# One 32-row product turned round: weights stationary in 128-column pieces instead of a product, a copy and four transposes

## The chip, the cores and the metric

One core of one Trainium2 chip runs the whole program. The metric is device time in microseconds of one execution; the kernel before took 707.13 us (median of three timed runs, 706.22 to 708.27). TensorE is written PE, its weight loads PEld, VectorE DVE, ScalarE ACT, GpSimd POOL and SyncE SP. SP issues all the transfers of this kernel.

## The reference

```python
def _attn_ref(x, state):                      # x (4, 8, 512, 64), state (4, 8, 32, 64)
    a = softmax(x @ state.T / 8);    xread = a @ state
    a2 = softmax(state @ x.T / 8);   sread = a2 @ x
    return concatenate([xread, sread], axis=2)          # 544 tokens for each of 4 batches
def _moe_ref(x, w_in, w_out, alpha):          # x (2176, 512), w_in (512, 2048), w_out (2048, 512)
    h = x @ w_in
    g = maximum(h, 0) + alpha * minimum(h, 0)
    return g @ w_out
def _moe2_ref(x, w_in, w_out):
    h = x @ w_in
    g = maximum(h, 0) + log1p(exp(-abs(h)))
    return g @ w_out
```

(The softmax lines are shortened.) The two stages are fed one from the other: attention, then stage 0 (with alpha), then stage 1. Each batch gives 512 token rows and 32 state rows; the state rows of the four batches together make one more block of 128 rows.

## The kernel before, in words

The work is cut by stage `m` (0 and 1), by quarter `q` of the 2048 hidden columns (512 each), by batch block `b` (0 to 3, 512 token rows each, and `b == B`, the 128 state rows), and by piece `fc` of 128 hidden columns. Most products are done three times on halves (`mm3`: high by high, high by low, low by high); some, the state rows' first product of stage 0 among them, are done once in full f32, which the trace shows as two passes for each matmul.

Stage 0 of the token blocks never multiplies `w_in` with the attention output. The product of state and `w_in` (`sw_products`, steps `w`) is made first and multiplied with the attention weights (`hidden` for `b < B`). For the state rows, `sr[0]` holds the 128 rows transposed, and their first product is with `w_in` itself (`whole(q, k)`, four row pieces `k`). The kernel before holds 128 columns of `sr` stationary and streams 512 columns of `w_in` (`hidden_rows`, L369). The result has tokens on its partitions, and the next product needs hidden columns there, so ACT copies it out (`rows_copy` L389, in quarter 0 step `J` L893), and PE transposes it in four pieces of 128 by 128 (`turned_rows` L397, in quarter 0 step `H` 16, by the helper at L633). Then `act` follows: a Relu on ACT (L413), `prelu` on DVE (L405), the split into halves (L184, L185). The second product of a block (`out_part`) runs three blocks later (`LAG = 3`).

Quarter 0 and the attention are written out by hand as the list `ORDER`: a letter is a step, a number its index, and every engine takes its own steps in the order of the list. The names that matter here: `N` filler transposes of the identity (L641), `L` loads of weights, `P` the load of alpha, `x` and `y` loads of the inputs `xt` and `xs`, `s` and `S` scores (L700), `b` 0 the transposition of group 0's weights (L633), `T`, `K`, `R`, `F`, `X` the state rows' own attention, `w` the products of state and `w_in` (L333), `H` first products, `A C G D` their activation. From quarter 1 on, Python loops write the order, and tables say beside which block further work is put: `TICKS` and `GROUP_TICKS` (conversion of one 128 by 512 weight tile: ACT L262 and L263, DVE L267 to L277, POOL L283, store and next load on SP), `W_AHEAD` and `Y_AHEAD` (preparation of stage 1). The second stage runs groups of seven products (`product`, L586).

The lines of quarters 1 to 3 around the state rows:

```python
for fc in range(4 if b < B else 1):
    hs = rows_copy(0, q) if b == B else None
    if n in TICKS[q]:
        conv_head()
    ps = hidden(0, q, b, fc) if b < B else turned_rows(hs, lambda: out_part(*todo.pop(0)))
    g = act(0, q, b, fc, ps)
    if len(todo) >= LAG:
        out_part(*todo.pop(0))
```

Of the kernel before, what the change touches and what calls it, by code (L numbers as in the profile page):

```python
# [49 lines left out]
b0 f1 x2 L4 Z0 N12 t1 v1 a2 j2 m1 f2 g1 x3 a3 K0 u1 N12 e1 v2 S2 j3 R0 z1 f3 r1 n1 L5 g2 k3 v3 k2 g3 N7 t2 B0 F0 w00  # L50
w01 t3 m3 b1 m2 a4 j4 e2 z2 u3 f4 p00 c0 e3 V0 X0 H0 r2 v4 p01 L6 a5 q01 n2 z3 g4 A0 W0 b2 j5 H1 c2 C0 d2 a6 A1 r3 h4
H3 d0 f5 H2 n3 G0 L7 N3 w03 C1 j6 G1 l4 L8 A2 c1 D0 D1 p03 x5 f6 C2 v6 v5 q03 b3 G2 A3 C3 c3 D2 g6 G3 g5 O0 D3 d3 w02
h5 p02 q02 d1 M2 x4 h6 a8 a7 j7 f7 M1 H5 l5 v7 S4 H4 E2 A4 j8 L9 A5 C5 C4 f8 y1 v8 O1 k4 M4 t4 E1 l6 g7 G4 k5 h7 l7 H6
D4 O2 G5 g8 y2 H7 L10 A6 a9 T2 T1 O3 D5 C6 j9 E4 m4 t5 m5 u5 f9 M5 v9 u4 a10 A7 Q3 e4 O4 z4 e5 r4 C7 z5 E5 K1 K2 O5 G6
Z2 r5 n4 R2 n5 Z4 D6 b4 M3 R1 T4 F2 Z1 F1 X2 b5 c5 c4 O6 W2 X1 y3 d4 G7 d5 Z5 E3 H8 x6 x7 W1 D7 j10 A8 f10 H9 K4 A9
L11 C8 T3 C9 G8 G9 K3 O7 Q7 S6 R3 Z3 H10 k7 D9 v10 T5 D8 t7 F3 m7 u7 k6 e7 X3 A10 t6 m6 O8 M6 K5 y4 L12 H11 y5 z7 C10
M7 u6 e6 W3 r7 E6 A11 G10 g10 g9 D10 R4 z6 r6 R5 F5 L13 n7 b7 O9 a11 C11 n6 c7 G11 b6 O10 F4 c6 a12 D11 y6 y7 L14 d6
T6 X5 W5 E7 j11 X4 f11 v11 d7 H12 g11 K6 H13 W4 A12 R6 a13 T7 A13 C12 Z7 j12 G12 Z6 C13 f12 O11 D12 H14 v12 G13 Q11
D13 g12 A14 F6 O12 H15 C14 j13 L15 G14 a14 K7 f13 X6 R7 W6 D14 h12 w11 F7 v13 j14 l12 g13 A15 a15 f14 C15 v14 j15 X7
L16 f15 W7 h13 O13 G15 g14 l13 O14 v15 D15 I0 w10 p11 J0 H16 A16 h14 g15 l14 q11 O15 C16 p10 q10 G16 D16 H17 L17 Q15  # L60
H18 A17 A18 O16 H19 w13 C17 h15 G17 C18 D17 G18 Q16 A19 H20 D18 O17 C19 G19 p13 A20 q13 w12 C20 D19 G20 p12 l15 D20
L18 q12
# [1033 lines left out]
```

## Time and profile before

| what | value |
|---|---|
| timed runs, median (lowest to highest) | 707.13 us (706.22 to 708.27) |
| the profiled execution, its own time | 705.88 us |
| span, first to last instruction of that execution | 704.1 us |
| busy: PE / PEld / DVE / ACT / POOL | 694.9 / 545.6 / 506.3 / 468.7 / 355.0 us |
| mean granted clock of TensorE | 1.000 of full speed |

The span is what the views of the trace divide up; 1.8 us lie around it. Busy time of PE counts pipelined matmuls with overlaps, so it says that PE has no long gaps and not that it is at its peak. The profiled execution is 1.25 us below the median.

### The profile page before, as it was taken

What the parts mean: (1) busy time and instruction counts of PE and PEld (TensorE: products, weight loads), DVE (VectorE), ACT (ScalarE), POOL (GpSimd) and SP (SyncE); (2) the same over time, 40 slices, a digit from 0 to 9 for tenths busy, and PEclk for the clock granted to TensorE, in tenths of its full rate; (3) what the DMA queues carried; (4) which work ended last, traced back from release to release, by engine and by line L of the source; (5) the groups of instructions that cost most, each with busy time, mean ns of one, the idle gap of its engine ahead of it and who ended that gap; (6) DMA issues with size and microseconds to landing.
All of it is one profiled execution on the core that took longest, in us unless ns stands there. A gap on an engine that the chain in (4) does not pass through costs nothing.

```text
span 704.1 us, 10175 instructions
## 1 busy us (share of the span) xinstructions
PE 694.9 (99%) x3512; PEld 545.6 (77%) x3512; DVE 506.3 (72%) x832; ACT 468.7 (67%) x921; POOL 355.0 (50%) x401
## 2 busy tenths in 40 slices
PE   8999999999999999999999999999999999999997
PEld 6468776777777777768888888888888888888886
DVE  5988876678999988887355666757676456677665
ACT  4878786646656566555589866757885776766551
POOL 2562323015234324548997684287997666554110
PEclk9999999999999999999999999999999999999999
DMA  8262712122543464664110423103105121200003
GB/s 301 104 208 86 237 45 85 60 89 89 184 133 119 137 220 145 202 198 147 30 61 13 167 75 106 45 1 103 47 31 168 58 89 31 91 30 31 0 31 119
DMA packets 30483, 72.47 MB, mean 103 GB/s; under 512 B 3552, under 2 KB 3552, under 8 KB 30432
## 3 DMA queue, kind: packets, MB, share of 16 engines
q1 hardware_dynamic: 30432, 71.83, 30.9%
q8 instruction: 27, 0.44, 0.3%
q14 instruction: 24, 0.20, 0.1%
HBM read 58.97 MB, written 12.85 MB: 102 GB/s over the span
## 4 chain that ended last, share of the span: by engine, by line
PE 92%; DMA 3%; DVE 1%; POOL 1%; ACT 1%; issue 1%; SPq 0%; POOLq 0%; ACTq 0%
PE pa L586 22%; PE pb L179 17%; PE pb L181 17%; PE pb L180 17%; PE pa L179 4%; PE pa L181 4%; PE pa L180 4%; PE pa L333 2%; PE pa L369 1%; DMA stg<-w2o 1%; DMA acc<-xt 1%; DMA wo4l<-wo 1%; PE pa L633 1%; PE pb L641 1%; PE pb L700 1%
## 5 line engine op out<-in xcount | busy, mean ns | idle before, releaser
L283 POOL TENSOR_TENSOR stg<-top,stg 128x512 f32<-128x512 bf16 x48 | 58.4, 1218 | 102.7 <-DVE stg L277 74.6
L608 DVE TENSOR_TENSOR acc<-pb,acc 128x512 f32<-128x512 f32 x112 | 74.5, 685 | 24.7 <-PE pb L181 23.8
L405 DVE SCALAR_TENSOR_TENSOR pa<-tmp,rest,pa 128x512 f32<-128x512 f32 (+1 forms) x80 | 53.0, 670 | 27.3 <-ACT tmp L413 14.8
L416 ACT ACTIVATE tmp<-pa 128x512 f32<-128x512 f32 x68 | 40.2, 594 | 34.8 <-DVE pa L489 23.3
L419 DVE SCALAR_TENSOR_TENSOR pa<-pa,tmp 128x512 f32<-128x512 f32 x68 | 46.8, 693 | 15.7 <-ACT tmp L418 15.3
L267 DVE SCALAR_TENSOR_TENSOR top<-stg,top 128x512 uint16<-128x512 uint16 x63 | 51.3, 816 | 8.1 <-ACT top L263 8.0
L262 ACT ACTIVATE exp<-stg 128x512 bf16<-128x512 bf16 x63 | 42.0, 669 | 20.6 <-DMA stg<-w2o 6.3
L263 ACT ACTIVATE top<-exp,top_bias 128x512 uint16<-128x512 uint16 x64 | 46.2, 722 | 9.6 <-POOL stg L283 4.9
L418 ACT ACTIVATE tmp<-tmp 128x512 f32<-128x512 f32 x68 | 42.3, 630 | 0.7
L417 ACT ACTIVATE tmp<-tmp 128x512 f32<-128x512 f32 x68 | 42.2, 629 | 0.7
L489 DVE TENSOR_TENSOR pa<-pa,wo2l 128x512 f32<-128x512 f32 x32 | 22.2, 695 | 25.4 <-PE pa L586 25.3
L277 DVE SCALAR_TENSOR_TENSOR stg<-stg,exp 128x512 f32<-128x512 uint32 x48 | 38.8, 810 | 1.0
L451 DVE TENSOR_TENSOR acc<-pb,acc 128x512 f32<-128x512 f32 x54 | 35.1, 683 | 4.3 <-PE pb L181 4.3
L413 ACT ACTIVATE tmp<-pa 128x512 f32<-128x512 f32 x47 | 27.4, 589 | 12.0 <-PE pa L181 6.6
L489 DVE TENSOR_TENSOR wo2h<-pa,wo2h 128x512 f32<-128x512 f32 x16 | 11.0, 690 | 27.9 <-ACT wo2h L1003 18.1
L185 POOL TENSOR_TENSOR ex1l<-at1h,ex1h 128x256 fp32r<-128x256 f32 x16 | 11.9, 746 | 32.6 <-ACT ex1h L184 26.3
L184 ACT ACTIVATE g1h<-pa 128x512 fp32r<-128x512 f32 x26 | 15.5, 596 | 19.3 <-DVE pa L405 10.9
L273 DVE TENSOR_SCALAR exp<-top 128x512 uint16<-128x512 uint16 x64 | 24.4, 381 | 1.0
L184 ACT ACTIVATE g0h<-pa 128x512 fp32r<-128x512 f32 x23 | 13.7, 595 | 13.8 <-DVE pa L405 11.7
L185 POOL TENSOR_TENSOR wo5l<-wo5l,wo5h 128x512 fp32r<-128x512 f32 x8 | 10.4, 1299 | 22.1 <-ACT wo5h L184 19.7
L489 DVE TENSOR_TENSOR wo2l<-pa,wo2h 128x512 f32<-128x512 f32 x16 | 11.0, 690 | 14.2 <-PE pa L586 14.1
L185 DVE TENSOR_TENSOR g2l<-pa,g2h 128x512 fp32r<-128x512 f32 x24 | 16.5, 687 | 6.5 <-ACT g2h L184 6.2
(808 smaller groups left out, 2450.3 us busy)
## 6 DMA issues: line engine op xcount, KB each, us to landing
stg<-w1o SPq DMA_DIRECT2D x16, 511.8 KB, 4.1
stg<-w2i SPq DMA_DIRECT2D x16, 511.8 KB, 4.4
stg<-w2o SPq DMA_DIRECT2D x16, 511.8 KB, 3.7
stg<-w1i SPq DMA_DIRECT2D x15, 511.8 KB, 4.4
acc<-xt SPq DMA_DIRECT2D x16, 256.0 KB, 5.0
wi<-stg SPq DMA_DIRECT2D x16, 256.0 KB, 3.6
wo<-stg SPq DMA_DIRECT2D x16, 256.0 KB, 2.3
out<-acc SPq DMA_DIRECT2D x16, 256.0 KB, 2.2
```

The lines of the kernel that those rows point to most:

```text
L179: nc.tensor.matmul(ps, lh, rh, start=start, stop=False)
L180: nc.tensor.matmul(ps, lh, rl, start=False, stop=False)
L181: nc.tensor.matmul(ps, ll, rh, start=False, stop=stop)
L263: nc.scalar.activation(t.bitcast(U16), e.bitcast(U16), AF.Relu, bias=top_bias, scale=TOP_SCALE)
L267: nc.vector.scalar_tensor_tensor(out=tu, in0=words(i)[0], scalar=TOP_SIGN, in1=tu, op0=ALU.bitwise_and, op1=ALU.bitwise_or)
L283: nc.gpsimd.tensor_tensor(out=a, in0=parts(i)[0], in1=a, op=ALU.add)
L405: nc.vector.scalar_tensor_tensor(out=ps[:, cs], in0=t[:, cs], scalar=a, in1=ps[:, cs], op0=ALU.mult, op1=ALU.add)
L418: nc.scalar.activation(t, t, AF.Ln, bias=1.0)
L419: nc.vector.scalar_tensor_tensor(out=ps, in0=ps, scalar=0.0, in1=t, op0=ALU.max, op1=ALU.add)
L489: eng.tensor_tensor(out=o, in0=x, in1=y, op=op)
L586: nc.tensor.matmul(ps, l[:, c], r, start=first and k == 0 and i == 0, stop=k == 1 and i == 2, skip_group_check=not first,)
L608: nc.vector.tensor_tensor(out=a, in0=ps, in1=a, op=ALU.add)
```

## The change

The state rows' first product in stage 0 is now made by `rows_by_columns`: for each of four pieces of 128 hidden columns and four row pieces, 128 by 128 of `w_in` is stationary and 128 columns of `sr` stream. The result has hidden columns on its partitions, as `act` takes it. `rows_copy`, `turned_rows` and the steps `I` and `J` go; stage 1 keeps its product, copy and transposes. Alpha's load (`P0`) goes from the second place of the queue to behind the fourth weight load. The list `ORDER` and the tables are written anew.

```diff
-L0 N1 N6 N5 N12 P0 U0 x0 s0 a0 N3 L1 j0 L2 k0 a1 x1 f0 v0 N3 t0 M0 m0 N4 g0 y0 L3 e0 N3 s1 j1 z0 r0 E0 n0 k1 N2 T0 N11
+L0 N3 N12 N3 N1 N5 N6 U0 x0 a0 s0 L1 x1 L2 k0 j0 a1 f0 v0 N6 t0 L3 M0 N4 m0 N1 s1 j1 P0 g0 E0 N3 N13 N14 f1 e0 z0 r0
...
-TICKS = {1: range(4, 17), 2: range(17), 3: range(11)}
-GROUP_TICKS = (0, 2, 1, 1, 1, 2, 0, 0)
+TICKS = {1: range(4, 17), 2: range(0, 17), 3: (0, 1, 2, 3, 5, 6, 7, 8, 9, 10, 11)}
+GROUP_TICKS = (0, 2, 1, 3, 0, 1, 0, 0)
...
-W_AHEAD = {4: 1, 5: 1, 6: 1, 7: 1, 8: 1, 9: 2, 10: 1, 11: 2}
-Y_AHEAD = {11: 2, 12: 2, 13: 2, 14: 2, 15: 1}
+W_AHEAD = {4: 2, 5: 1, 6: 1, 8: 1, 10: 4, 12: 1}
+Y_AHEAD = {11: 1, 12: 3, 13: 3, 16: 2}
...
-    def hidden_rows(m, q):
+    def hidden_rows(q):
 
         ps = bank(psa)
         for k in range(4):
             c = slice(k * P, (k + 1) * P)
-            if m == 0:
-                nc.tensor.matmul(ps, sr[0].f[:, c], whole(q, k), start=k == 0, stop=k == 3)
-            else:
-                xh, xl = R(sr)
-                mm3(ps, xh[:, c], xl[:, c], *R(nat[k]), k == 0, k == 3)
+            xh, xl = R(sr)
+            mm3(ps, xh[:, c], xl[:, c], *R(nat[k]), k == 0, k == 3)
+        return ps
+
+    def rows_by_columns(q):
+
+        ps = bank(psa)
+        for fc in range(4):
+            f = slice(fc * P, (fc + 1) * P)
+            for k in range(4):
+                x = sr[0].f[:, k * P : (k + 1) * P]
+                nc.tensor.matmul(ps[:, f], whole(q, k)[:, f], x, start=k == 0, stop=k == 3)
         return ps
...
-        return turned_rows(rows_copy(m, q))
-
-    def rows_copy(m, q):
-        ps = hidden_rows(m, q)
+        if m == 0:
+            return rows_by_columns(q)
+        ps = hidden_rows(q)
         hs = tslot()
         nc.scalar.activation(hs, ps, AF.Copy)
-        return hs
-
-    def turned_rows(hs, between=None):
-        if between:
-            between()
         ps = bank(psa)
         for c in range(4):
             nc.tensor.transpose(ps[:, c * P : (c + 1) * P], hs[:, c * P : (c + 1) * P], ident)
...
-                live["H", i] = bank(psa)
-                turned(live["H", i], live["J"])
-
-        @step
-        def I_(i):
-            live["I"] = hidden_rows(0, 0)
-
-        @step
-        def J(i):
-            live["J"] = tslot()
-            nc.scalar.activation(live["J"], live["I"], AF.Copy)
+                live["H", i] = rows_by_columns(q)
...
-                hs = rows_copy(0, q) if b == B else None
                 if n in TICKS[q]:
                     conv_head()
-                ps = hidden(0, q, b, fc) if b < B else turned_rows(hs, lambda: out_part(*todo.pop(0)))
+                ps = hidden(0, q, b, fc)
```

PE, quarter 3, the state rows (`srh` holds their transposed rows, `wi2h` to `wi3l` the four row pieces of `w_in`, `tmp` the copy; the operand streamed stands first behind the arrow). Before:

```order
L181 MATMUL pa_2900<-at3h,sw3l 128x512
L369 MATMUL pa_2937<-wi2h,srh 128x512
L369 MATMUL pa_2937<-wi2l,srh 128x512
L369 MATMUL pa_2937<-wi3h,srh 128x512
L369 MATMUL pa_2937<-wi3l,srh 128x512
L179 MATMUL pb_2911<-g3h,wo5h 128x512
...
L181 MATMUL pb_2914<-g0h,wo6l 128x512
L397 MATMUL pa_2957<-ident,tmp_71 128x128 x4
L179 MATMUL pa_2981<-at4h,sw4h 128x512
```

The same place of the changed kernel:

```order
L181 MATMUL pa_2920<-at3h,sw3l 128x512
L379 MATMUL pa_2955<-srh,wi2h 128x128
L379 MATMUL pa_2955<-srh,wi2l 128x128
L379 MATMUL pa_2955<-srh,wi3h 128x128
L379 MATMUL pa_2955<-srh,wi3l 128x128
L179 MATMUL pb_2931<-g3h,wo5h 128x512
L180 MATMUL pb_2931<-g3l,wo5h 128x512
L181 MATMUL pb_2931<-g3h,wo5l 128x512
L379 MATMUL pa_2955<-srh,wi2h 128x128
```

Four matmuls of 512 streamed columns and four transposes become sixteen matmuls of 128 streamed columns, with second-stage products put between them; nothing on PE stands behind a copy there any more.

PE at the start of the program (`acc_99` to `acc_104` are the places of the inputs `xt`, `pb_224` the filler's bank). Before:

```order
L700 MATMUL pb_296<-acc_102,ex0h 32x512 x2
L641 MATMUL pb_224<-ident 128x128 x2
L633 MATMUL pa_310<-ident,ex0l 128x128 x4
L641 MATMUL pb_224<-ident 128x128 x11
L633 MATMUL pb_326<-ident,acc_100 128x128 x4
L641 MATMUL pb_224<-ident 128x128 x24
L700 MATMUL pb_377<-acc_103,ex0h 32x512
```

The same place of the changed kernel:

```order
L701 MATMUL pb_295<-acc_102,ex0h 32x512 x2
L642 MATMUL pb_224<-ident 128x128 x30
L634 MATMUL pb_340<-ident,acc_100 128x128 x4
L701 MATMUL pb_357<-acc_103,ex0h 32x512
L701 MATMUL pb_358<-acc_99,ex0h 32x512
```

The filler that stood between step `b` 0 (which frees `acc_100` for the next input) and the scores `S` 2 now stands ahead of `b` 0, and the transposes of step `T` 0 have moved behind `S` 2.

## Rows read from the trace of the kernel before

**Rows 1.** The page: busy time by engine, and the granted clock in 40 slices.
```profile
PE 694.9 (99%) x3512; PEld 545.6 (77%) x3512; DVE 506.3 (72%) x832; ACT 468.7 (67%) x921; POOL 355.0 (50%) x401
PEclk9999999999999999999999999999999999999999
```
**Rows 2.** The waits of PE over the whole span: total us, times, longest us.
```profile
PE pa L397 <- ACT tmp L389: 1.7, 1, 1.7
...
PE pb L700 <- DMA acc<-xt: 0.9, 2, 0.5
...
PE pa L333 <- DVE g0l L912: 0.7, 1, 0.7
```
**Rows 3.** Busy time by stretch: length, PE, PEld, DVE, ACT, POOL, clock, DMA.
```profile
37.30:300.00 262.70, 262.66 (x1520) 197.86 (x1514) 220.17 (x370) 174.57 (x338) 92.22 (x79) 1.00 0.42 137
```
**Rows 4.** The timeline of PE around 308 us: start, us, operation.
```profile
305.89 0.39 PE L180 MATMUL pb<-g0l,wo6h 128*128 128x512 f32 x1
306.12 0.39 PE L181 MATMUL pb<-g0h,wo6l 128*128 128x512 f32 x1
308.19 0.66 PE L397 MATMUL pa<-ident,tmp 128*128 128x128 f32 x4 [1.68 <-ACT tmp L389]
308.60 0.48 PE L179 MATMUL pa<-at4h,sw4h 128*128 128x512 f32 x1
```
**Rows 5.** The timeline of ACT in the same stretch.
```profile
306.99 0.67 ACT L262 ACTIVATE exp<-stg 128x512 bf16<-128x512 bf16 x1 [1.09 <-DMA stg<-w2o]
307.55 0.58 ACT L389 ACTIVATE tmp<-pa 128x512 f32<-128x512 f32 x1
308.94 0.58 ACT L413 ACTIVATE tmp<-pa 128x512 f32<-128x512 f32 x1
```
**Rows 6.** The chain that ended last: one product of the state rows.
```profile
108.94 3.43 PE pa L369 x8
```
**Rows 7.** L369, its weight loads: ns min/median/max, first and last start.
```profile
L369 PEld LDWEIGHTS pa<-wi0h,srh x4: 187/188/188, 108.6 to 220.5; 128*128 128x128 f32 x4
```
**Rows 8.** L397, weight loads of the transposes.
```profile
L397 PEld LDWEIGHTS pa<-ident,tmp x28: 137/139/143, 152.2 to 502.8; 128*128 128x128 f32 x28
```
**Rows 9.** The timeline of PE at 29 us.
```profile
28.97 0.60 PE L633 MATMUL pb<-ident,acc 128*128 128x128 f32 x4
29.41 1.02 PE L877 MATMUL pa<-wo4h,sw0h 128*128 128x512 f32 x2
30.27 0.59 PE L877 MATMUL pa<-wo4l,sw1h 128*128 128x512 f32 x1
```
**Rows 10.** The timeline of the weight loads at 29 us.
```profile
28.81 0.52 PEld L633 LDWEIGHTS pb<-ident,acc 128*128 128x128 f32 x4 [0.51 <-POOL acc L764]
29.30 0.30 PEld L877 LDWEIGHTS pa<-wo4h,sw0h 128*128 128x128 f32 x2
```
**Rows 11.** The timeline of PE in the first 36 us.
```profile
1.36 5.00 PE L641 MATMUL pb<-ident 128*128 128x128 f32 x24 [1.36 <-POOL ident masks.py:199]
...
15.33 0.66 PE L633 MATMUL pb<-ident,acc 128*128 128x128 f32 x4
15.82 2.78 PE L641 MATMUL pb<-ident 128*128 128x128 f32 x24
18.54 2.10 PE L700 MATMUL pb<-acc,ex0h 64*32 64x512 f32 x16
...
35.71 1.04 PE L333 MATMUL pa<-wi0h,ex0h 64*32 64x512 f32 x2 [0.66 <-DVE g0l L912]
```
**Rows 12.** The timeline of the transfers' queue on SP.
```profile
1.17 0.42 SPq L651 DMA_DIRECT2D alpha<-al  x1
...
16.05 0.33 SPq L664 DMA_DIRECT2D acc<-xt  x1
```
**Rows 13.** The timeline of DVE at 35 to 36 us.
```profile
34.98 0.68 DVE L912 TENSOR_TENSOR g0l<-pa,g0h 128x512 fp32r<-128x512 f32 x1
36.18 0.28 DVE L273 TENSOR_SCALAR exp<-top 128x512 uint16<-128x512 uint16 x1
```

More of the change, by code (lines that the diff above doesn't have):

```diff
@@ L48 @@
 ORDER = """
-L0 N1 N6 N5 N12 P0 U0 x0 s0 a0 N3 L1 j0 L2 k0 a1 x1 f0 v0 N3 t0 M0 m0 N4 g0 y0 L3 e0 N3 s1 j1 z0 r0 E0 n0 k1 N2 T0 N11
[L50 to L62, printed above, removed]
+L0 N3 N12 N3 N1 N5 N6 U0 x0 a0 s0 L1 x1 L2 k0 j0 a1 f0 v0 N6 t0 L3 M0 N4 m0 N1 s1 j1 P0 g0 E0 N3 N13 N14 f1 e0 z0 r0
+n0 b0 k1 x2 x3 y0 Z0 t1 a2 S2 v1 j2 m1 N1 u1 f2 g1 a3 L4 L5 T0 e1 N1 K0 j3 z1 f3 v2 N5 R0 r1 n1 g2 k3 B0 v3 k2 g3 N8
@@ new lines @@
+t2 w00 w01 t3 a4 m3 m2 b1 j4 e2 z2 f4 p00 c0 F0 V0 N3 X0 L6 u3 r2 e3 p01 H0 v4 a5 q01 n2 z3 b2 j5 A0 H1 g4 c2 a6 C0 d2
+H3 N1 W0 f5 A1 h4 G0 d0 r3 H2 w03 j6 n3 C1 x5 L7 G1 l4 f6 D0 A2 L8 D1 v6 v5 C2 p03 c1 G2 b3 q03 A3 C3 c3 g5 g6 D2 O0
+G3 d3 D3 M2 w02 h5 p02 q02 l5 y1 x4 h6 a7 j7 f7 M1 H5 v7 S4 H4 a8 A4 j8 C4 A5 k4 E2 C5 O1 y2 f8 L9 v8 M4 l6 g7 G4 H6
+E1 h7 l7 D4 k5 g8 G5 A6 O2 a9 t4 H7 L10 T2 C6 t5 O3 T1 j9 d1 f9 D5 E4 v9 Z2 m4 u4 m5 M5 K2 a10 u5 Q3 e4 A7 E5 z4 O4 e5
+r4 C7 G6 K1 z5 O5 r5 n4 n5 D6 M3 Z4 b4 R2 R1 T4 F2 Z1 c4 F1 X2 b5 W2 K4 c5 O6 X1 y3 d4 E3 d5 H8 x6 G7 x7 Z3 W1 A8 j10
@@ new lines @@
+f10 D7 H9 A9 L11 C8 Z5 T3 K3 C9 G8 O7 G9 Q7 D8 S6 R3 v10 H10 k7 D9 k6 T5 t7 F3 m7 u7 X3 e7 L12 y4 K5 A10 H11 O8 t6 m6
+y5 M6 g10 z7 u6 C10 E6 e6 M7 W3 r7 A11 G10 D10 R4 z6 r6 R5 F5 g9 n7 b7 L13 O9 a11 C11 n6 c7 F4 d7 O10 b6 G11 c6 a12
+D11 y6 y7 L14 d6 T6 X5 W5 E7 X4 j11 f11 v11 Z6 H12 g11 W4 K6 H13 A12 R6 T7 A13 C12 G12 a13 j12 Z7 C13 f12 O11 H14 D12
+G13 v12 Q11 D13 g12 A14 H15 j13 C14 O12 G14 K7 F6 h12 a14 L15 f13 X6 R7 W6 D14 w11 F7 X7 j14 p11 A15 v13 g13 f14 l12
+a15 h13 W7 j15 v14 L16 O13 g14 f15 v15 C15 l13 O14 H16 w10 g15 G15 A16 D15 h14 l14 q11 O15 p10 q10 C16 G16 H17 L17 Q15
@@ L63 @@
+H18 A17 D16 O16 h15 A18 H19 w13 C17 G17 C18 D17 G18 Q16 A19 H20 D18 C19 p13 O17 w12 G19 A20 C20 p12 q13 D19 L18 G20
+q12 D20 l15
 """.split()
```

## The prediction

> **What bounds the kernel now.** The page comes first [rows 1]: PE is busy for 694.9 of 704.1 us, no other engine for more than 506.3, and the granted clock is full in all 40 slices. That much busy time overlaps itself, so the next view is PE's own waits [rows 2]: over the whole span the longest is 1.7 us, for the copy L389 ahead of the transposes L397; the transfers of `xt` cost 0.9 us and one activation 0.7. The table by stretch [rows 3] shows the middle of the program with PE busy in 262.66 of 262.70 us. So from about 37 us on PE sets the time, and a change is worth what it takes off PE's stream or out of its few waits. DVE, ACT and the transfers count where PE waits for them, and that is in the first 37 us and at 308 us. All sums below are for the profiled execution, 705.88 us: its span of 704.1 and the 1.8 around it. It lies 1.25 us under the timed median of 707.13, and I add that at the end.
>
> **The transposes.** Stage 0 makes the state rows' product four times, once a quarter, and each has four transposes, 16 in all; the stage 1 ones stay. A run of four passes takes from 28.97 to 29.41 us, 0.44 us or 110 ns each, on its way to the next matmul [rows 9]. Sixteen of them are **-1.76 us**, on PE's stream and so on the path.
>
> **The wait for the copy.** In quarter 3 PE ends its last product at 306.51 (306.12 and 0.39) and begins to transpose at 308.19 [rows 4]; the wait is 1.68 us. ACT shows why [rows 5]: the copy stands behind a conversion that waited until 306.99 for a weight tile, and runs at 307.55. Without copy and transposes PE goes on to the next product at once. What stays late is the Relu of the state rows (L413, at 308.94 before [rows 5]). PE next needs its result in `out_part`, which runs three blocks later; a block is 6 first products and 12 second ones, and these come 0.23 us apart [rows 4], so about 4 us a block and 12 us of cover. **-1.7 us**. If that cover were gone, the wait would return as PE's wait for a `g` tile, and this term would be nothing. No other copy shows as a wait of PE [rows 2], so the other three cost it nothing, and that ACT is rid of four times 0.58 us [rows 5] gives nothing more.
>
> **The product itself.** Before, one product is eight passes of 512 columns in 3.43 us [rows 6], 429 ns each; four products are 13.73 us. After, it is 32 passes of 128 columns, each with a weight load of its own. The streamed columns are the same, so at 429 / 4 = 107 ns a pass nothing changes; the question is whether a load hides behind a pass this short. A full f32 load is recorded with 188 ns [rows 7], a transpose's with 139 [rows 8]. The trace has no such stream, so I bound it. Below: the transposes also bring a new stationary operand for each 128 columns and go at 110 ns, although their loads are recorded with 139. Above: the whole record exposed, 188 ns. The row that is nearest is at 29 us: a full f32 load begins at 29.30, behind the last transpose, and its matmul begins at 29.41, 110 ns after [rows 9, 10]; the two passes that it opens end on time, since the next begins at 30.27, 0.86 us later, which is two times 429. So one load of the right kind hides behind one pass of the right length. I take 112 ns: 128 passes x 0.112 = 14.3, **+0.6 us**. At 110 it would be +0.35, at 188 (24.1 us) +10.3. Second-stage products that now stand between the pieces have loads of the same length behind short passes, and 308.60 in [rows 4] begins 0.41 after four transposes began, so they add nothing that I could see.
>
> The Trainium skill has a rule against this form: TensorE: Matmul & The Clock Gate, section "Back-to-back issue gap", gives about 81 ns for each matmul of 128 columns in a stream of load and matmul, where the streaming alone would be 56. Put on top of 110 ns, those 25 would make +3.5 us of this term and a sum of about nothing; the 110 ns at 29 us speak against it, for one load.
>
> **The start.** Until 35.71 us PE runs fillers and waits [rows 11]; there it waited 0.66 us for `g0l` of DVE (34.98 and 0.68 [rows 13]), and then it never stops. The steps up to that point are the same in both kernels, so the start is worth what this one moment moves. (a) Alpha's issue at 1.17 took 0.42 us of the queue ahead of `st` and `xt` [rows 12]; these are issued that much earlier, and the scores wait for them [rows 2]: up to -0.4 for the chain behind. Alpha itself is now the tenth transfer, far ahead of its first use in an activation. (b) 30 fillers now stand ahead of step `b` 0 and none behind. Before, `b` 0 began at 15.33, the transfer that it frees was issued at 16.05 [rows 12], and the scores `S` 2 began at 18.54, with 24 fillers between them [rows 11]. The transfer sets that time; after, the first half of `S` 2 can run while it is under way, and only the second half waits. PE stands idle there for up to 2 us where it ran fillers. (c) `T` 0 comes behind `S` 2, so the copies that follow on ACT queue up some 0.5 us later, and DVE makes the maximum of group 2 before another transposition. (d) On DVE one more conversion piece of 0.28 us [rows 13] stands ahead of `g0l`. The gains in (a) and (b), about 0.4 each, and the losses in (c) and (d) are of one size: I take **0**, with -0.6 and +1.0 as ends.
>
> **The tables.** The conversions are 48 in both, one moved off the second block of quarter 3 and two from late groups of stage 1 into an earlier one; the stage 1 preparations are the same ones, moved by a block or two. What hides them is the idle time of ACT and POOL, busy for 67% and 50% [rows 1], and the three blocks ahead at which `g` tiles are made. **0**, and up to +1.5 if one of them makes PE wait.
>
> Sum: -1.76 - 1.7 + 0.6 + 0 = -2.85 us. 705.88 becomes 703.0, and the median 707.13 becomes **704.3 us**.
>
> **Rivals.**
> 1. Loads partly exposed: if loads follow each other at the recorded 139 ns of a transpose's load [rows 8], the term is 128 x 0.139 - 13.73 = +4.1 and the sum +0.6: 707.7 us, no change. For it: no row shows more than one such load in a row. Against it: the transposes go at 110 ns with that very record. The rule of the Trainium skill above, TensorE: Matmul & The Clock Gate, "Back-to-back issue gap", would end near here.
> 2. Loads wholly exposed, the one that ends slower: 188 ns a pass [rows 7], +10.3, sum +6.9: 714.0 us. It decides from 134 ns on, where the gains are used up, (13.73 + 3.46) / 128, and is slower by 0.3% from 151 ns. Against it is the start at 29.41 [rows 9, 10].
> 3. The clock falls in the idle time at 16 to 18 us. The first 24 fillers took 5.00 us and 24 later ones 2.78 [rows 11]: 208 against 110 ns, the lower of the two levels and the upper one. Before, no wait of PE behind that is longer than 1.7 us [rows 2], so no row shows what 2 us do. If it falls, the price is at most what the beginning lost, 2.2 us: the sum is -0.65, 706.5 us, no change.
> 4. The wait for the copy comes back elsewhere, behind the same late weight tiles: -2.85 + 1.7 = -1.15, 706.0 us, no change. For it: ACT's conversions still wait for those tiles. Against it: 12 us of cover.
> 5. The start ends 1 us earlier, and the timed runs, which lie 1.25 us above the profiled one, lose 1 us more of wait than it shows: 702.3 us.
>
> **Chances.** Two runs of this kernel differ by up to 0.3%, 2.1 us, which is about what a measurement tells from no change; faster then means below 705.0, slower above 709.2. The forecast has 0.54, rival 5 0.07, rival 1 0.10, rival 3 0.08, rival 4 0.09, rival 2 0.06, and a new wait from the tables that makes it slower 0.06. Some of rival 4's and the start's outcomes still end below 705.0 and some of the forecast's end above it; these cancel. So faster 0.61, same 0.27, slower 0.12. The range runs from just under rival 5 to rival 1, 702.2 to 707.7; rival 2 and the new wait, 0.12 together, lie beyond it, and some of what lies around its two ends.
>
> **What the profile after would show.** The passes of L379 110 to 113 ns apart, 256 records of load and matmul in all, no L389 copy before stage 1, and no wait of PE at 300 to 310 us. The first run without gaps on PE begins at 35.7, give or take a microsecond. In the waits, `xt` may show up to 2 us at 16 to 18 us. Wrong it would be by passes further apart than 134 ns, by a start later by more than a microsecond, by a granted clock below full after 6 us, or by a wait of PE between 300 and 370 us for a tile that ACT or POOL prepares late.

## The result and the profile after

The changed kernel takes 711.02 us (median of 5 runs, 709.86 to 714.4), the kernel before 707.13 (5 runs, 705.1 to 708.27): a ratio of 1.0078 with a 95% interval from 1.0058 to 1.0099. It is slower by 0.8%, clear of the noise; the forecast was 704.3 and the range ended at 707.7. The profiled execution takes 710.23 us, its span 708.4, against 705.88 and 704.1 before.

The page of the changed kernel, the lines that answer to [rows 1]:

```profile
PE 695.4 (98%) x3598; PEld 554.9 (78%) x3598; DVE 509.2 (72%) x832; ACT 466.4 (66%) x917; POOL 357.0 (50%) x401
PEclk9999999999999999999999999999999999999999
```

PE is as busy as before, and the clock looks full, but each digit stands for 17.7 us and hides what follows. The waits of PE, as in [rows 2]:

```profile
PE pb L701 <- DMA acc<-xt: 2.5, 1, 2.5
PE pa L333 <- DVE g0l L903: 2.4, 1, 2.4
PE pb L179 <- DVE acc L452: 2.1, 1, 2.1
```

The wait for the copy is gone. The one for L452 is new, and those for `xt` and `g0l` have grown: before, the longest were 0.5 and 0.7 us [rows 2]. The table by stretch shows them with the clock that was granted (columns as in [rows 3]):

```profile
35.00:45.00 10.00, 7.62 (x47) 3.44 (x47) 8.99 (x14) 5.37 (x11) 5.56 (x5) 0.83 0.63 210
45.00:300.00 255.00, 255.00 (x1540) 199.17 (x1539) 209.22 (x355) 165.73 (x325) 83.83 (x70) 1.00 0.40 128
300.00:320.00 20.00, 17.86 (x89) 15.15 (x87) 17.89 (x32) 11.28 (x21) 10.91 (x13) 0.91 0.49 157
```

Between 45 and 300 us PE never stops, as before. Two places lose: around 37 us and behind 300 us, each with a wait and with a granted clock of 0.83 and 0.91 of full speed on the mean.

**The product.** PE's instructions of L379 by operands (ns min/median/max, first and last start), and PE's timeline at the state rows of quarter 3:

```profile
L379 PE MATMUL pa<-srh,wi0h x16: 270/275/275, 111.9 to 228.7; 128*128 128x128 f32 x16
L379 PE MATMUL pa<-srh,wi2h x16: 270/275/422, 146.5 to 309.4; 128*128 128x128 f32 x16
```

```profile
299.92 0.38 PE L379 MATMUL pa<-srh,wi2h 128*128 128x128 f32 x2
300.14 0.39 PE L379 MATMUL pa<-srh,wi2l 128*128 128x128 f32 x2
...
303.11 0.47 PE L179 MATMUL pb<-g3h,wo5h 128*128 128x512 f32 x1 [2.14 <-DVE acc L452]
...
303.88 0.56 PE L379 MATMUL pa<-srh,wi2h 128*128 128x128 f32 x2
```

Two passes start 0.22 us after two others: 110 to 112 ns a pass, with its weight load hidden. The maximum of 422 ns and the 0.56 at 303.88 are passes at the lower clock: the granted clock is 0.58 from 304 to 308 us.

**The start.** PE's timeline where before it has 35.71 and a wait of 0.66 [rows 11], and DVE's for the steps ahead of `g0l`, which was at 34.98 [rows 13]:

```profile
18.94 1.05 PE L701 MATMUL pb<-acc,ex0h 64*32 64x512 f32 x6 [2.54 <-DMA acc<-xt]
37.78 1.06 PE L333 MATMUL pa<-wi0h,ex0h 64*32 64x512 f32 x1 [2.38 <-DVE g0l L903]
```

```profile
34.33 1.53 DVE L267 SCALAR_TENSOR_TENSOR top<-stg,top 128x512 uint16<-128x512 uint16 x1 [0.23 <-issue]
35.78 0.74 DVE L406 SCALAR_TENSOR_TENSOR pa<-tmp,rest,pa 128x512 f32<-128x512 f32 x1
36.44 0.69 DVE L273 TENSOR_SCALAR exp<-top 128x512 uint16<-128x512 uint16 x1
37.05 0.68 DVE L903 TENSOR_TENSOR g0l<-pa,g0h 128x512 fp32r<-128x512 f32 x1
```

`g0l` comes 2.07 us later, and the matmuls behind the wait last 1.06 us, where they are done in 0.61 at the full clock (e12 below). Stretch by stretch, the clock is full up to 37 us and 0.50 of full speed, the lower of its two levels, from 38 to 41 us.

**Quarter 3.** The queue of SP in the changed kernel, then the same place of the kernel before, then ACT of the changed kernel and, last, of the kernel before:

```profile
283.95 0.38 SPq L312 DMA_DIRECT2D wo<-stg  x1
288.25 0.33 SPq L244 DMA_DIRECT2D stg<-w2i  x1
288.63 0.42 SPq L505 DMA_DIRECT2D wo4l<-wo  x1
```

```profile
280.56 0.32 SPq L312 DMA_DIRECT2D wo<-stg  x1
280.93 0.43 SPq L504 DMA_DIRECT2D wo4l<-wo  x1
285.07 0.33 SPq L244 DMA_DIRECT2D stg<-w2i  x1
```

```profile
293.27 0.63 ACT L184 ACTIVATE wo4h<-wo4l 128x512 fp32r<-128x512 f32 x1 [4.31 <-DMA wo4l<-wo]
293.81 0.58 ACT L184 ACTIVATE g2h<-pa 128x512 fp32r<-128x512 f32 x1
```

```profile
285.63 0.63 ACT L184 ACTIVATE wo4h<-wo4l 128x512 fp32r<-128x512 f32 x1 [1.42 <-DMA wo4l<-wo]
```

The weight load L244 waits on SP until the store ahead of it has landed (its data has arrived), 3.8 us. Before, the load of `wo4l` stood ahead of it, and now it stands behind. ACT waits 4.31 us for it (1.42 before) with `g2h` next in its queue. DVE of the changed kernel, then of the kernel before:

```profile
294.43 0.69 DVE L185 TENSOR_TENSOR g2l<-pa,g2h 128x512 fp32r<-128x512 f32 x1 [3.33 <-ACT g2h L184]
302.29 0.68 DVE L452 TENSOR_TENSOR acc<-pb,acc 128x512 f32<-128x512 f32 x1
```

```profile
298.89 0.68 DVE L451 TENSOR_TENSOR acc<-pb,acc 128x512 f32<-128x512 f32 x1
```

DVE waits 3.33 us for `g2h`, its work behind that is late, and the taking out (L452, L451 before) comes 3.4 us later. It empties the place that PE writes next, and PE waits 2.14 us for it.

### The profile page after: what moved, and what is told of

Its sections match the earlier page's. It is cut to its first block, busy times and chain, and to the rows that moved or that the text cites. A ratio compares the mean times of both kernels' runs of the same rounds, so it can differ in the third digit from the quotient of the medians.

```text
span 708.4 us, 10342 instructions
## 1 busy us (share of the span) xinstructions
PE 695.4 (98%) x3598; PEld 554.9 (78%) x3598; DVE 509.2 (72%) x832; ACT 466.4 (66%) x917; POOL 357.0 (50%) x401
## 4 chain that ended last, share of the span: by engine, by line
PE 95%; DVE 3%; DMA 1%; issue 1%; ACT 0%; POOL 0%; POOLq 0%; SPq 0%; DVEq 0%
PE pa L587 22%; PE pb L179 17%; PE pb L181 17%; PE pb L180 17%; PE pa L179 5%; PE pa L180 4%; PE pa L181 4%; PE pa L333 2%; PE pa L379 2%; PE pb L642 2%; DMA wo4l<-wo 1%; PE pa L826 1%; DVE top L267 1%; PE pa L634 1%; DMA acc<-xt 0%
## 5 line engine op out<-in xcount | busy, mean ns | idle before, releaser
L267 DVE SCALAR_TENSOR_TENSOR top<-stg,top 128x512 uint16<-128x512 uint16 x63 | 53.9, 857 | 15.5 <-ACT top L263 15.2
L452 DVE TENSOR_TENSOR acc<-pb,acc 128x512 f32<-128x512 f32 x54 | 35.0, 681 | 3.9 <-PE pb L181 3.9
L185 POOL TENSOR_TENSOR wi4l<-at0h,wi4h 128x256 fp32r<-128x256 f32 x16 | 11.9, 745 | 27.0 <-ACT wi4h L184 24.5
L184 ACT ACTIVATE g3h<-pa 128x512 fp32r<-128x512 f32 x22 | 13.1, 594 | 14.2 <-DVE pa L406 14.2
```

What stands on the lines that cost most here:

```text
L184: a = nc.scalar.activation(h, src, AF.Copy) if eng_h is nc.scalar else eng_h.tensor_copy(h, src)
L267: nc.vector.scalar_tensor_tensor(out=tu, in0=words(i)[0], scalar=TOP_SIGN, in1=tu, op0=ALU.bitwise_and, op1=ALU.bitwise_or)
```

## The experiments

In each trace I compare the ends of the same passes of the three-pass products (L179 to L181), counted from the first. The table gives the end of five of them and of the span, in us later (+) or earlier (-) than in the profile of the kernel before, where they stand at the time in the head; the last two columns are the ratio of the runs to the kernel before on the same chip, with its interval, and the runs from fastest to slowest.

| | 66.1 | 108.7 | 126.4 | 281.5 | 310.0 | end | ratio | runs, us |
|---|---|---|---|---|---|---|---|---|
| changed kernel | 3.12 | 3.11 | 2.85 | 2.40 | 4.27 | 4.32 | 1.0078 (1.0058-1.0099) | 709.9-714.4 |
| e1 | 0.73 | 0.73 | 2.06 | 1.54 | 7.13 | 6.93 | 1.0108 (1.0092-1.0125) | 711.6-714.8 |
| e2 | 3.82 | 3.81 | 6.22 | 6.26 | 4.37 | 4.17 | 1.0067 (1.0054-1.0081) | 708.9-710.8 |
| e5 | 2.48 | 2.48 | 2.22 | 1.76 | -0.22 | -0.41 | 1.0038 (1.0022-1.0054) | 705.5-711.3 |
| e6 | 3.69 | 3.71 | 3.45 | 4.60 | 3.91 | 3.70 | 1.0061 (1.0048-1.0074) | 708.8-710.1 |
| e7 | 0.08 | 0.09 | 1.41 | 1.75 | 1.05 | 0.84 | 1.0028 (1.0015-1.0041) | 706.4-708.4 |
| e8 | 0.17 | 0.23 | 0.24 | 0.24 | 0.13 | 0.14 | 1.0005 (0.9995-1.0015) | 704.7-706.9 |
| e9 | 0.86 | 0.86 | 0.60 | 0.12 | -1.83 | -2.05 | 1.0025 (1.0006-1.0044) | 703.8-709.5 |
| e15 (e9 again) | 0.59 | 0.60 | 0.34 | -0.07 | 3.04 | 2.83 | one run | 708.7 |
| e16 (e9 again) | 1.59 | 1.63 | 1.37 | 0.97 | -0.43 | -0.64 | one run | 705.2 |
| e10 | 1.05 | 1.07 | 0.81 | 0.35 | 1.93 | 1.72 | 1.0044 (1.0024-1.0065) | 705.8-712.3 |
| e11 | 3.84 | 3.86 | 3.59 | 3.12 | 2.39 | 2.17 | 1.0053 (1.0034-1.0071) | 706.8-712.5 |
| e12 | 2.23 | 2.23 | 1.97 | 1.52 | 1.07 | 0.86 | 1.0038 (1.0024-1.0052) | 705.4-709.6 |
| e13 | 0.97 | 1.01 | 0.75 | 0.60 | 0.09 | -0.08 | 0.9995 (0.9984-1.0007) | 703.6-706.5 |
| e14 | 1.50 | 1.50 | 1.24 | 0.81 | 0.11 | -0.11 | 1.0037 (1.0018-1.0055) | 704.9-710.1 |
| e17 | 1.30 | 1.29 | 1.03 | 0.72 | -1.47 | -1.61 | 0.9994 (0.9985-1.0002) | 703.5-704.5 |
| e18 | 3.55 | 3.54 | 3.28 | 2.86 | 5.10 | 4.99 | 1.0073 (1.0054-1.0092) | 707.0-711.5 |

The kernel before ran from 703.3 to 708.5 us on these chips, with medians of 704.5 to 705.4 but for the first result's 707.1. A profile is one execution and can lie 3 us and more off its kernel's median; so the columns of times tell where a wait stands, and the ratio what the kernel costs. Where a diff below names no other kernel, it is against the changed kernel; `...` marks what is left out.

**e1, the product alone**, with the order (without the steps `I0` and `J0`) and all tables of the kernel before.

```diff
-TICKS = {1: range(4, 17), 2: range(0, 17), 3: (0, 1, 2, 3, 5, 6, 7, 8, 9, 10, 11)}
+TICKS = {1: range(4, 17), 2: range(17), 3: range(11)}
...
-L0 N3 N12 N3 N1 N5 N6 U0 x0 a0 s0 L1 x1
+L0 N1 N6 N5 N12 P0 U0 x0 s0 a0 N3 L1 j0
```

> The product by columns alone, with the order of the start and the tables of before. My theory is that the change lost in two places that are not the product: the start's new order made the low half of the first converted tile late (2.1 us of wait, then about 1.1 us at the lower clock), and SP's queue took the load of wo4l behind a weight load that waits for a store (2.1 us of wait in quarter 3, then about 1.5 us at the lower clock). By it the start's loss goes and the other stays, since SP's order is the changed one here too: 707.1 - 2.85 + 3.6, about 707.9 us, with w03 at 35.7 us again and a wait of about 2 us of TensorE for the VectorE's taking out in quarter 3. First rival: the moved ticks and preparations (tables) make the wait in quarter 3; then it is gone here and the time is about 704.3 us. Second rival: the product by columns costs more than its passes show; then the time is above 709 us with no such wait.

712.84 us. The start's loss is gone (0.73 at 66 us) and the wait in quarter 3 is there, larger than I expected:

```profile
PE pb L178 <- DVE acc L451: 5.1, 1, 5.1
```

So the moved ticks and preparations are not what makes this wait; with the old ones it is 5.1 us. Another 1.3 us are lost between 109 and 126 us, with a wait of 0.5 us for `g3l`; that the old order does not fit the new product there is my reading and was not tried.

SP's queue shows what the product alone moved. Up to 290 us it differs from that of the kernel before, in this kernel as in the changed one, by five swaps of neighbours (in the kernel before near 181, 242, 258, 276 and 283 us); the last is that of `wo4l`. In e2, with the old product and the new tables, none of the five stands.

**e2, the order and the tables alone**, with the product, copy and transposes of before.

```diff
-                live["H", i] = rows_by_columns(q)
+                live["H", i] = bank(psa)
+                turned(live["H", i], live["J"])
...
-H16
+I0 w10 J0 H16
```

> The start's new order and the new tables, with the old product, its copy and its transposes (alpha's load late too). By my theory the start's loss of 3.2 us stands here and the wait for wo4l in quarter 3 does not, since SP's order has wo4l ahead of the weight load: 707.1 + 3.2, about 710.3 us, w03 at 37.8 us. By the first rival (the tables make the wait in quarter 3) both losses stand: about 713.9 us. By a third rival, that the start's loss is made up for before the end since what follows it waits anyway, about 707 us.

710.53 us, as the theory said, by other parts: 3.8 us late at 66 us, 2.4 more between 109 and 126 us, and then no wait at 308 us, since PE comes there 6 us later than before.

**e3 and e4, the load of wo4l first.** e4 is the same on e1. Both leave out more than was meant: the second half's loads of the output weights (from about 310 us on), because `(q, c) not in got` also skips those. So their times say nothing of the whole kernel.

```diff
-            wload()
+            with tc.issue_after(ahead["SP"]) if ahead else nullcontext():
+                wload()
...
+    def wo_first():
...
+        got[0, 1] = nc.sync.dma_start(out=lo.bitcast(F32), in_=kept_w["o", 1, 0, 1]).ins
+        ahead["SP"] = got[0, 1]
...
-        nc.sync.dma_start(out=t, in_=kept_w["o", 1, q, c])
+        if (q, c) not in got:
+            got[q, c] = nc.sync.dma_start(out=t, in_=kept_w["o", 1, q, c]).ins
...
+                if last_q and n == 2:
+                    wo_first()
```

> The changed kernel, with the load of wo4l put ahead of the weight load on SP's queue, as it stands in the kernel before; nothing else is changed by hand. By my theory ACT then waits no 4.3 us for wo4l in quarter 3, TensorE's wait of 2.1 us and the lower clock behind it go: 711.0 - 3.6, about 707.4 us. By the first rival (the tables' moved work) the wait stays and so does the time, 711 us. Between them: the wait goes but the late work of ACT comes back as another wait of 1 to 2 us some microseconds later, as at the state rows' copy in the kernel before: about 709 us.

> The product by columns with the start and the tables of before, and the load of wo4l ahead of the weight load on SP. By my theory both losses are undone and only the product's own terms stay: 707.1 - 2.85, about 704.3 us, faster than both kernels. By the second rival (the product costs more than it shows) 707 us or more. If the wait only moves (to another tile that ACT makes late), 705.5 to 706.5 us.

Measured 707.61 and 710.53 us. Up to 310 us both do all the work: in e3 the wait of quarter 3 shrinks to 0.2 us, in e4, with the old tables and the old order, 4.0 us of it stay. The late load of `wo4l` is thus not its only cause; the new tables and the rest of the new order take the other part away (e9 below has no such wait).

**e5, the same on the changed kernel, with every load.**

> The changed kernel with the one load of wo4l ahead of the weight load on SP's queue, every load done (e3_after_wo4_first and e4_product_alone_wo4_first left out the second half's loads of the output weights, whose results are not used here). My theory: the wait of 2.1 us in quarter 3 and the lower clock behind it go and nothing else changes, 3.3 us less than the changed kernel, a ratio to the kernel before of about 1.003. Rival: e3_after_wo4_first gained by the loads that it left out in the second half, not by the order; then this one stands at the changed kernel's 1.0078.

SP's queue and ACT in e5:

```profile
283.14 0.43 SPq L494 DMA_DIRECT2D wo4l<-wo  x1
```

```profile
288.96 0.63 ACT L184 ACTIVATE wo4h<-wo4l 128x512 fp32r<-128x512 f32 x1 [1.71 <-DMA wo4l<-wo]
```

707.56 us, ratio 1.0038: the wait and the lower clock in quarter 3 are gone (from 1.76 to -0.22 between 281 and 310 us, where the changed kernel goes from 2.40 to 4.27). By the ratios, this one place in SP's queue is worth 0.4% with the new start.

**e6 and e7, every store ahead of the weight loads**, on the changed kernel and with the old start's order throughout.

```diff
+        if wsrc[i][1] == 1:
+            kept = nc.sync.dma_start(out=kept_w[wsrc[i][:4]], in_=rounded[i]).ins
+            stored.add(wsrc[i][:4])
         while nload[0] < len(wsrc) and may_load(nload[0]):
-            wload()
+            with tc.issue_after(kept) if wsrc[i][1] == 1 else nullcontext():
+                wload()
         if wsrc[i][1] == 1:
-            nc.sync.dma_start(out=kept_w[wsrc[i][:4]], in_=rounded[i])
-            stored.add(wsrc[i][:4])
```

> The changed kernel with every store of a converted tile issued on SP ahead of the weight loads of its turn, so that a load no longer stands in front of the next store while it waits for the landing of the last one; wo4l falls ahead of its weight load too. In the profiles with the new product a load and a store take turns from 238 us on, some 4.3 us a turn. My theory, wider than before: it is these turns that make the converted tiles late, and wo4l is only the last of them; then the wait in quarter 3 goes here as in e5, ratio about 1.003, and SP's issue of wo3l comes at about 275 us and not at 279.7. Rival: the loads now wait for POOL's sums instead (the store ahead of them waits for POOL), come later, and ACT waits for weight tiles: ratio 1.008 or more.

> The start's order of before with the new product and the new tables, and the stores ahead of the loads as in e6. My theory: the start's loss (3.2 us in the profiles) and quarter 3's are both gone and the product's terms stay: 0.996, about 702.5 us where the kernel before gives 705.4. Rival, from e4 (old start, old tables, wo4l ahead, 4.0 us of wait in quarter 3 still): it is the old start that makes quarter 3 late with the new product, so a wait of 2 us or more stands here and the ratio is 1.002 or more. If the old tables were the cause in e4, no wait stands here.

1.0061 and 1.0028. The theory fell in both; e6 lies between theory and rival, and e7 has its rival's ratio with half of the wait that this named. SP issues `wo3l` at 283.4 us in e6, later than the 279.7 of the changed kernel, since a load now stands behind a store that waits for POOL. PE's wait in quarter 3 is 1.0 us in both profiles, and the runs of either lie within 2 us.

**e8, the kernel before with wo4l behind the weight load** (`behind[51]`, the load of the 52nd weight tile; the diff is against the kernel before).

```diff
+        with tc.issue_after(behind[51]):
+            return nc.sync.dma_start(out=lo.bitcast(F32), in_=kept_w["o", 1, 0, 1]).ins
```

> The kernel before, with only the load of wo4l put behind the weight load on SP, as the changed kernel has it; the four loads behind it stay behind it. My theory: ACT's first half of wo4 comes some 3 us later, what stands behind it on ACT comes late, and TensorE waits about 2 us in quarter 3 and then runs at the lower clock for some 3 us: plus 3 us, ratio about 1.004. Rival: without the shorter product ACT is early enough, and the lateness is taken up in front of the state rows' copy, where 1.7 us are waited anyway: within 1 us, ratio 1.000 to 1.0015.

1.0005, no change: the rival held. ACT's timeline of this kernel says why it proves less than it seems:

```profile
285.32 0.60 ACT L184 ACTIVATE g2h<-pa 128x512 fp32r<-128x512 f32 x1 [0.71 <-DVE pa L406]
289.67 0.64 ACT L184 ACTIVATE wo4h<-wo4l 128x512 fp32r<-128x512 f32 x1 [3.75 <-DMA wo4l<-wo]
```

ACT waits 3.75 us for `wo4l`, but the compiler's order has put `g2h` ahead of that wait. So either this or the old product spares it; e8 does not tell the two apart, and e11 speaks for the first.

**e9 and e10, the start's order of before**, up to `d3`; e9 with `wo4l` first as in e5.

```diff
-L0 N3 N12 N3 N1 N5 N6 U0 x0 a0 s0 L1 x1 ... D3
+L0 N1 N6 N5 N12 P0 U0 x0 s0 a0 N3 L1 j0 ... d3
```

> The changed kernel with two places undone: the order of the start up to d3 (some 50 us, alpha's early load with it) is that of before, and wo4l's load stands ahead of the weight load on SP as in e5. The product, the rest of the order and the tables are the new ones. My theory: only what I forecast of the product is left, the transposes (-1.76), the passes (+0.6) and the wait for the copy (-1.7): 0.996 of the kernel before, about 702.3 us at 705.2, no wait of TensorE behind 20 us over 1 us. Rival, from e7 and e1: the old start does not fit the new product, and a wait of some 1 us at 111 us and of 1 to 4 us in quarter 3 takes the gain, ratio 1.001 or more.

> The changed kernel with the order of the start alone undone up to d3. My theory: w03 comes at about 35.7 us again, TensorE's clock does not fall there, 3.1 us less than the changed kernel up to 66 us; the wait in quarter 3 with its lower clock stays (3.9 us between 281 and 310 us where the kernel before has 1.9): 1.0035 (1.0078 less 3.1 us of 705). Rival: the start's loss is only shifted, since ACT and VectorE are ahead by less in quarter 3 when TensorE is early, and the wait there grows by what the start gained: 1.006 to 1.008.

The start's loss is gone: 0.9 and 1.1 at 66 us instead of 3.1, and what is left there is a wait for `xt` at 44 us, which stands where the old and the new order meet. The wait of quarter 3 stays in e10:

```profile
PE pb L179 <- DVE acc L452: 1.9, 1, 1.9
```

e10 gains 0.34% of the 0.78. e9's profiled execution took 703.83 us, 2 us less than the profile of before, but its 12 runs reach from 703.8 to 709.5, and the median of 707.26 is slower than before. e9 and e10 differ by `wo4l`'s place alone, 1.0025 against 1.0044 with intervals that overlap: with the old start, the runs do not show this one swap to be worth anything.

**e11, ACT's first half of wo4 later**, SP's order left (`third[3, 4]`, ACT's last instruction of the fifth block of quarter 3).

```diff
-        split(nc.scalar, nc.gpsimd, hi, lo, t)
+        with tc.issue_after(third[3, 4]) if nwo[0] == 2 else nullcontext():
+            split(nc.scalar, nc.gpsimd, hi, lo, t)
```

> The changed kernel, SP's order left as it is (wo4l behind the weight load); on ACT the first half of wo4 stands behind g2h, g3h and the cuts of wi4 and wi5, and no longer ahead of g2h. In e8 ACT's order had moved too (wo4h behind g2h), so that run did not tell what the late load costs where g2h stands behind it. My theory: it is the 4.3 us for which ACT stands before wo4h with g2h and g3h behind it that costs; wo4l may be late. Then the wait in quarter 3 and the lower clock go here as in e5, ratio 1.003 to 1.004. Rival: the converted tiles come late from SP's turns whatever ACT's order; then TensorE still waits 2 us there and the ratio stays at 1.007.

1.0053, between the two, with an interval that overlaps that of the changed kernel. In the profile PE's wait in quarter 3 falls from 2.14 to 1.14 us and the clock stays full there, 2.6 us less between 281 and 310 us than in the changed kernel; the start lost 0.7 us more in this profile.

**e12, fillers in the wait ahead of w03.**

```diff
-w03
+N20 w03
```

> The changed kernel with 20 transposes of the identity (2.2 us, result unused) in front of w03, in TensorE's wait of 2.4 us for the low half of g0; nothing comes earlier by them. If the lower clock behind that wait comes from TensorE having been idle, as I think, w03's passes take 0.43 us and not 0.6 to 1.06, and the kernel gains the clock's part alone, 0.8 to 1.1 us at 44 us: ratio 1.0065. If the clock falls there for another reason, it falls here too and the time stays at 1.0078; and if the fillers end after g0's low half has come, up to 0.2 us is lost.

PE's timeline of this kernel at 37 us, then the stretch from 36 to 42 us in the changed kernel and in e12 (columns as in [rows 3]):

```profile
35.38 2.35 PE L642 MATMUL pb<-ident 128*128 128x128 f32 x20
37.77 1.04 PE L333 MATMUL pa<-wi0h,ex0h 64*32 64x512 f32 x2
38.37 0.61 PE L333 MATMUL pa<-wi1h,ex0h 64*32 64x512 f32 x1
```

```profile
36.00:42.00 6.00, 4.22 (x22) 1.86 (x23) 5.76 (x10) 2.67 (x6) 3.27 (x3) 0.72 0.59 175
```

```profile
36.00:42.00 6.00, 5.95 (x43) 3.98 (x42) 5.97 (x10) 3.55 (x8) 3.27 (x3) 1.00 0.61 177
```

`w03` starts no earlier (37.77 against 37.78), and yet the kernel is 0.9 us further at 66 us: the granted clock from 36 to 42 us is 1.00 here and 0.72 in the changed kernel. That the clock falls behind PE's idle time there, and that this is worth 0.9 us, is shown; in e2, e3, e5, e6 and e11, which have the same wait of 2.4 us, it falls too. The ratio gained more, 1.0038; quarter 3 had a wait of only 1.4 us in this profile.

**e13 to e16, where e9's runs spread.** e13 undoes the last three of SP's five swaps and leaves those near 181 and 242 us, so it is not quite SP's whole order of before; e14 joins the edits of e9 and e11; e15 and e16 are e9 once more. The edit of e13, as SP's queue in the changed kernel (-) and in e13 (+); e9 has the last of the three swaps already:

```diff
-stg_64<-w1o
 wi_193<-stg_65
+stg_64<-w1o
...
-wo_196<-stg_65
 wo3l<-wo_186
+wo_196<-stg_65
...
-stg_66<-w2i
 wo4l<-wo_187
+stg_66<-w2i
```

> The kernel of e9 (old start, new product, rest of the order and tables new) with SP's whole order in quarters 2 and 3 as in the kernel before: the store of wi_193 ahead of the load of w1o, wo3l ahead of the store of wo_196, wo4l ahead of its weight load. If SP's turns are what makes e9's executions spread, they spread here no more than those of before (3 us) and the median is 702.5 to 703.5 us where before gives 705.1, ratio 0.997. If the start makes the spread, it stays: ratio 1.001 to 1.003.

> The kernel of e9 with ACT's first half of wo4 behind g2h, g3h and the cuts of wi4 and wi5 too, as in e11. If the executions of e9 that take 707 us and more wait in quarter 3 for ACT standing before wo4h, they are gone here: median 703 to 704 us, ratio 0.998. If they lose elsewhere, ratio 1.002.

> The kernel of e9 once more, one execution for its profile. If it takes 707 us or more, its trace shows the place: a wait of TensorE of 2 us or more in quarter 3 if SP's turns are the cause, or one ahead of 50 us, for xt or behind it with the lower clock, if it is the start.

> As e15, one more execution, since either may fall among those near 704 us.

e15 fell among the long ones, 708.74 us, and shows the place. The waits of PE in e15; the queue of SP in e9, then in e15:

```profile
PE pb L179 <- DVE acc L454: 3.1, 2, 2.7
```

```profile
281.53 0.42 SPq L494 DMA_DIRECT2D wo4l<-wo  x1
285.78 0.33 SPq L244 DMA_DIRECT2D stg<-w2i  x1
```

```profile
282.53 0.42 SPq L494 DMA_DIRECT2D wo4l<-wo  x1
288.29 0.33 SPq L244 DMA_DIRECT2D stg<-w2i  x1
```

It is the same program. From the store ahead of L244 to its landing SP waited 1.5 us longer (5.3 us in e15, 3.8 in e9), SP handed that on to everything behind, and PE waits 2.7 us and then runs at the lower clock, where e9 waits nothing. e16 took 705.24 us and has no wait in quarter 3 either. With two more swaps undone than in e9 (e13) the runs lie within 2.9 us and the median is 704.44, ratio 0.9995, not the 0.997 expected; a wait of 1.4 us stands in quarter 3 there. With ACT's order changed on top of e9 (e14) the spread stays. So the spread comes from those swaps in SP's order; how it arises is read from one long execution.

**e17, the stores issued by POOL.**

```diff
-            nc.sync.dma_start(out=kept_w[wsrc[i][:4]], in_=rounded[i])
+            nc.gpsimd.dma_start(out=kept_w[wsrc[i][:4]], in_=rounded[i])
```

> The kernel of e10 (old start, new product, rest of the order and tables new) with the stores of the converted tiles issued by POOL, which makes them, and not by SP. A load on SP then waits for the landing of its own place's store alone, no other store stands behind it. If SP's turns hold the wait of quarter 3, it is gone in every execution, and the product's gain shows: 702 to 703 us where before gives 705, a spread of no more than 3 us, ratio 0.996. Rival: POOL's issue of a store costs it time (a microsecond or more each, 32 of them), its sums come late and the loss is larger than the gain: ratio 1.002 or more.

704.06 us, ratio 0.9994, and all 11 runs within 1 us. The first of the waits of PE in this kernel:

```profile
PE pa L701 <- DMA acc<-xt: 1.4, 1, 1.4
```

No wait of PE stands in quarter 3 any more. But the edit moved two things: with the stores gone from SP, the compiler also put `wo4l` ahead of its weight load again (281 against 290 us on SP), as in e9. Against e9, which has that too, the stores' move takes the spread from 5.7 to 1.0 us and the ratio from 1.0025 to 0.9994. The 0.996 expected did not come. POOL pays 0.56 us for an issue, 32 times, and has the room (53% busy). The Trainium skill, DMA: Bandwidth & Descriptors, section "Issuing engines are not separate DMA queues", says that issuing from several engines saves only the time of issuing; here it also took the stores, and the waits for their landing, out of the way of loads that had nothing to do with them. The 1.3 us that this kernel is late at 66 us, by the `xt` wait where the two orders meet, stay; with `x4` issued earlier it might beat the kernel before, which was not tried.

**e18, j6 and f6 behind the low half of g0.**

```diff
-w03 j6 n3 C1 x5 L7 G1 l4 f6 D0 A2 L8 D1
+w03 n3 C1 x5 L7 G1 l4 D0 j6 f6 A2 L8 D1
```

> The changed kernel with the two steps j6 and f6 on VectorE behind D0, the low half of g0, and not ahead of it. If it is these two that make g0's low half late (0.7 and 1.5 us in the trace), w03 starts at about 35.7 us as before, the clock does not fall there, and the landmark at 66 us is 3 us earlier than in the changed kernel; the end gains less, as the wait in quarter 3 takes what TensorE is early: ratio 1.004. If what is late is C0 and what feeds it (0.6 us), w03 starts no earlier than 37 us.

The wait moved by one tile. PE's timeline:

```profile
36.43 1.04 PE L333 MATMUL pa<-wi0h,ex0h 64*32 64x512 f32 x2 [0.37 <-DVE g0l L903]
38.72 1.06 PE L333 MATMUL pa<-wi1h,ex0h 64*32 64x512 f32 x1 [1.25 <-DVE g1l L903]
```

`g0l` comes 1.4 us earlier, but `g1l` now stands behind the two steps, PE waits for that, and the clock falls as before: 3.55 at 66 us. So the two steps account for 1.4 of the 2.07 us, but another place for them on DVE only hands the lateness to the next tile. Which of the start's moves makes DVE as a whole late there is open.

## Why the prediction was wrong

**The product: right.** 112 ns a pass were forecast and measured; a load recorded with 188 to 192 ns is hidden behind every pass at the full clock, in quarter 0 in 32 passes in a row, and rivals 1 and 2 fall. The 25 ns a pass, my estimate from the Trainium skill, TensorE: Matmul & The Clock Gate, section "Back-to-back issue gap" (81 less 56 ns), do not show in these rows. Transposes and passes together, forecast at -1.16, come to about -0.9: 0.26, 0.19 and 0.26 us in the first three products, as the times at neighbouring passes show. The fourth lies in the wait of quarter 3; e9, which has no wait there, gives 0.27 for it.

**The wait for the copy, -1.7: failed.** I called the cover of 12 us enough because I looked only at what the Relu of the state rows feeds. PE did lose that wait, and waited 5 us earlier for the taking out L452, 2.14 us. In outcome this is rival 4, to which I gave 0.09; but the lateness is another, since ACT stood for `wo4l` and not for the weight tiles that rival 4 names. So the step that failed is the assumption that nothing else would hold PE in quarter 3. The term itself was there to be had: with `wo4l` ahead and the old start (e9), the profile gains 1.95 us between 281 and 310 us, the whole wait and the fourth product. Over the kernels the wait differs with their orders: 5.1 us in e1, 4.0 in e4, 1.4 in e13, none in e5, e9 and e17. Of the signs that I had named, three came: "a wait of PE between 300 and 370 us for a tile that ACT or POOL prepares late" (at 301, by DVE), a start later by more than a microsecond, and a clock below full after 6 us.

**The tables and the queue, 0 and up to +1.5: failed, by something that I did not look at.** e1 clears the tables of the wait. What cost is that with the new product the compiler set SP's queue in another order, five swaps up to 290 us, one of which put `wo4l` behind a load that waits for a landing. I read the order of PE, and of SP only at the start. With the old start, undoing the last three swaps takes the ratio from 1.0044 (e10) to 0.9995 (e13), 0.5%, and the start itself is the other part, from 1.0078 to 1.0044. `wo4l`'s swap alone gave 0.4% with the new start (e5) and nothing clear of noise with the old one (e9). That it costs by what stands behind it on ACT fits e8 and e11, and no run separates it from all else.

**The start, 0 with ends at -0.6 and +1.0: failed.** It is +3.1 us: 2.07 of later `g0l`, and about 0.9 of lower clock behind the wait (e12). The order as a whole is the cause (e9, e10), and (c) and (d) of the forecast had the right sign at less than half of the size. Which step of the order makes `g0l` late stays open (e18).

**Rival 3, the clock at 16 to 18 us.** I gave it 0.08, and it comes in five of the eight profiled executions that have this start up to there. In the changed kernel's profile PE is idle for 2.54 us there and the clock stays full, as behind 2.32 us in e12 and 2.07 in e5. It falls behind 1.92 to 2.10 us in e2, e3, e6, e11 and e18. The stretch in e11 (columns as in [rows 3]), PE in e11, then PE in e5:

```profile
20.00:26.00 6.00, 5.91 (x69) 3.73 (x67) 3.50 (x6) 3.90 (x7) 3.58 (x4) 0.76 0.76 281
```

```profile
18.08 1.06 PE L703 MATMUL pb<-acc,ex0h 64*32 64x512 f32 x6 [2.08 <-DMA acc<-xt]
38.36 1.04 PE L334 MATMUL pa<-wi0h,ex0h 64*32 64x512 f32 x2 [2.38 <-DVE g0l L905]
```

```profile
18.32 1.05 PE L710 MATMUL pb<-acc,ex0h 64*32 64x512 f32 x6 [2.07 <-DMA acc<-xt]
37.16 0.83 PE L335 MATMUL pa<-wi0h,ex0h 64*32 64x512 f32 x1 [2.39 <-DVE g0l L912]
```

The same start and almost the same wait: from `S` 2 to `w03` it is 20.28 us with the fall and 18.84 without, as in the changed kernel's profile, so the fall costs 1.4 us. The times at 66.1 us part the executions in the same way: 2.23 to 3.12 us late without it, 3.55 to 4.42 with it (4.42 in e3, which is not in the table). How often it falls in the changed kernel's timed runs is not known; its profile escaped it.

The profile's own sum: +3.1 at the start, -0.9 for the products, +2.1 in quarter 3 (its wait and clock less the wait of before) and next to nothing after it, together 4.3 us, which is the difference of the spans.

## What to carry to other kernels

A shorter product on the engine that sets the time changes more than its own instructions: where a compiler orders the queues, compare the order of every queue, SP's above all, before giving a moved step no cost. A transfer that waits for a landing holds all transfers behind it on its queue, and the engine that waits for one of those holds its own queue; what that costs went, in these runs, by the most urgent step behind the wait. A wait that vanishes in one place of a kernel whose supply is late can come back at another tile, as in e13 and e18; see that the supply is early before counting the wait as won.
